# A planned attention and gMLP kernel: late weight loads moved behind the last key copy, GpSimd stepped by the planner as an engine of its own, smaller probability buffer, first query tile ahead of the first key tile

## The chip, the cores and the metric

The kernel runs on one core of one Trainium2 chip. The metric is the device time of one execution in microseconds (us); lower is better. Engines are named as in the profile: PE is the tensor engine (PEld its weight loads), ACT the scalar engine, DVE the vector engine, POOL is GpSimd, and SP only issues DMAs (SPq is its queue). PSUM is the matmul's output memory, in eight banks of 512 float32 columns.

## The reference

```python
# S = 2048 tokens, D = 512, 32 heads of 16; one key head and one value head for all
q = (x @ wq) in 32 heads; k = x @ wk; v = x @ wv          # k, v: [2048, 16]
a = softmax(q k^T / 4) v, heads side by side, @ wo
z = gelu(x @ w_in); z1, z2 = z[:, :688], layernorm(z[:, 688:])
b = (z1 * (w_sp @ z2 + b_sp)) @ w_out                     # w_sp: [2048, 2048]
out = sigmoid(x . gate_w) * a + (1 - sigmoid(x . gate_w)) * b
```

The attention has 32 x 2048 x 2048 scores, and each needs an exponential.

## The kernel before, in words

**Units and blocks.** The attention is cut into 32 units. A unit is 512 queries (chunk c = unit // 8) and four heads, one per group of 32 partitions. Units come in pairs that share one tile of queries, `QA`; the second unit of a pair reads its heads 16 partitions further down. That is why the keys stand twice in `KA`: `KA[:, 0]` comes from the key projection, and `KA[:, 1]` is the same data shifted by 16 partitions, which a DMA makes from `KA[:, 0]` (`ld_K1`, line 306, one DMA for each of the four chunks of 512 keys). Odd units read the shifted copy. A block is one head's 512 queries against 128 keys: one score matmul (`ps<-QA,KA`), 128x512 values. There are 64 blocks in a unit, 2048 in all.

**Two ways to the exponential.** Most blocks go to ACT, which takes the exponential of two (sometimes three or one) PSUM banks in one instruction (line 804) into `P`, a ring of `PB` tiles of 512 columns. Other blocks, up to eight key tiles of each unit, go to DVE in batches of four: `A` (line 816) reads the scores from PSUM and writes a linear function of them to `UW[:, 0]`; `u` (line 823) squares it in place; `W` (line 829) squares once more into `UW[:, 1]`. The rest of the polynomial is done by PE, with sums of the keys and values (`KTV`, `SVB`) made once. W reads and writes SBUF alone, so POOL may do it too; POOL then takes pieces of 256 columns, one or two at a time, and DVE takes what is left. PE multiplies P, u and W by the values (`ps<-P,V`, `ps<-UW,V`, `ps<-UW,VW`) into one PSUM bank, and these matmuls run four at a time on 32 columns each (a round).

**After a unit.** DVE transposes the unit's sums (`T1`, line 841) and takes the reciprocal of the row sums; POOL scales a pair of units (`Tn`, line 869) into a buffer for the whole chunk; when a chunk's eight units are done, SP issues a DMA transpose of it into `OT` (`t2_dma`, line 877). PE multiplies `OT` by `wo` in the output groups `g_out`, with the gMLP part of the same rows.

**The gMLP branch** fills PE between the attention's steps: z2 and z1 from `win`, gelu on ACT in one stretch (187 to 211 us), layernorm statistics and scaling on DVE (lines 635 and 649), and then, for each of four chunks of 512 rows, the product with `w_sp` (`g_sp`, line 687 on DVE). Its right side `wT` is loaded by four DMA transposes for each chunk (`ld_wT`, line 339). The next chunk's four are put on SP when the last product of the chunk before has been planned, and they overwrite what that product reads.

**The order of the work** is made by a planner in the Python code, before anything runs. It keeps a clock for PE, ACT and DVE, and always steps the engine whose clock is furthest behind: `pe_step`, `act_step` and `dve_step` choose the next instruction by rules and costs in ns and write it to that engine's list. `T[...]` holds the time at which the planner believes something ready. Every engine then runs its list strictly in order, with semaphores for the true dependences. So a belief of the planner that is wrong is paid as a wait, and everything behind the waiting instruction in its engine's list waits as well. Some beliefs that matter here: a shifted key copy is ready 2.95 us after the planner sends it to SP (`ld_K1`: 650 ns of SP's time and 2300 ns), whatever else stands in SP's list; `OT` is ready 7 us after `Tn` (`C_T2`).

**SP's list.** DMAs of one list issue in order, and an instruction that waits holds all behind it. `sp_dma` chains by default: each such DMA waits until the one chained before it has landed. The loads of `wo` (eight DMAs), `wout` and the first `wT` (`ld_wo`, `ld_rest`) are put on SP in `done` of `g_KTV` (lines 588 to 595).

**POOL in the planner.** `pool_try` is called only at the start of a DVE step. It looks at how much PSUM reading DVE has ahead of it (`psum_work`); while DVE reads PSUM, POOL may use SBUF without meeting DVE's two-input squares. A piece of two (512 columns) is given when that work is at least 1000 ns, a piece of one at 560 ns, only after 64 us of the plan, and not between the start of the gelu stretch and the end of the layernorm. `lock` makes the planner charge a DVE square for what is left of a POOL instruction.

Of the kernel before, what the change touches and what calls it, by code (L numbers as in the profile page):

```python
# [22 lines left out]
LN_EPS = 1e-5  # L23
PB = 19
ND = 5
# [12 lines left out]
DBK = (5, 4)  # L38
# [14 lines left out]
WPOOL = True  # L53
C_PW = 1000.0
C_ZN = 1200.0
ZP = ()
C_PH = 580.0
# [112 lines left out]
def build_kernel(nc, x_d, wq_d, wk_d, wv_d, wo_d, win_d, wsp_d, bsp_d, wout_d, gw_d, out_d):  # L170
    es = ExitStack()
    with es:
# [35 lines left out]
        rc = sb("rc", [128, 2, 16], F32)  # L208
        Tn = sb("Tn", [128, 2, 512], B16)
        OT = sb("OT", [128, 2, 16, 128], B16)  # L210
# [34 lines left out]
        TB = [outsb[:, :, :].rearrange("p k n -> p (k n)"), winf[:, 0:2048], winf[:, 2048:4096], winf[:, 0:2048]]  # L245
        TBK = [[("ob", k) for k in range(4)], ["W0"], ["W1"], ["W0"]]
        OT3 = winf[:, 4096:4608]
        wo3 = winf[:, 4608:5120]
# [195 lines left out]

        def g_K(c, lo=0, hi=512, b=BM):
            key = "K0a" if c == XO[0] and lo == 0 else ("K0", c)

            def piece(dt):
                return lambda: fm(b, hi - lo, 0, wk_rep[:, dt, :], xT[:, dt, 512 * c + lo:512 * c + hi], dt == 0, dt == 3, ["wk_rep", ("x", c)], "K")

            def ev():
                op("dve", lambda v: v.tensor_copy(KA[:, 0, 512 * c + lo:512 * c + hi], bank(b, hi - lo)), r=[bkey(b)], w=[key], tag="Kev")
# [15 lines left out]
            return Group([((hi - lo) / 2.4 + 2.6, piece(dt)) for dt in range(4)], [(68.0 + (hi - lo) / 0.96, ev)], lambda: when(("x", c)), done, bank=b, tag="K")  # L468

# [104 lines left out]
        def g_KTV():  # L574
            n0 = NKT - NMAX

            def piece(k, e):
                def f():
                    for q in range(4):
                        o = 512 * BM + 32 * NMAX * e  # L580
                        mm(ps[32 * q:32 * q + 32, o:o + 32 * (k + 1)], KN[:, k, e, :], V1[:, n0 + k:n0 + k + 1, :].broadcast_to([128, k + 1, 32]), k == NMAX - 1, k == 0,
                           ["KN", ("V", (n0 + k) // 4)], [bkey(BM)], tp=(0, 32 * q), tag="KTV")
                return f

            def ev():
                op("dve", lambda v: v.tensor_scalar(KF, bank(BM, 64 * NMAX).rearrange("p (e k w) -> p k e w", e=2, w=32), Q_C1, None, ALU.mult),
                   r=[bkey(BM), ("z1", 5)], w=["KF"], tag="KTVev")

            def done(t):
                for q in range(4):  # L590
                    op("sp", lambda d, q=q: d.dma_start(KTV[32 * q:32 * q + 32, :, :, q, :], KF[32 * q:32 * q + 32, :, :, :]),  # L591
                       r=["KF", ("z1", 5)], w=[("KTV", q)], dma=16, after=[o_ktv], tag="KTV")
# [253 lines left out]
        def norm_ops(pgx, c, jp, jjs, b0=0, b1=16, t1k=None, eng="dve", big=False):  # L846
# [16 lines left out]
            def d():  # L863
                dst = TB[c].rearrange("p (b z j w) -> p z j b w", z=4, j=2, w=16)[:, jp, :, :, :] if big else tnv[:, pr, j0:j1, b0:b1, :]
                aft = list(pgx.ops["dve"][-2:-1]) if eng == "pool" else []
                if big and c and jp == 0:
# [3 lines left out]
                                                      rc[:, j0:j1, b0:b1].unsqueeze(3).broadcast_to([128, n, nb, 16]), ALU.mult),  # L870
                       r=t1k + [("rc", j, b0) for j in jjs], w=TBK[c] if big else [("Tn", pr, j, b0) for j in jjs],
                       after=aft, tag="Tn")
# [77 lines left out]
        for i, c in enumerate(XO):  # L950
# [643 lines left out]
        def lock(now):  # L1594
            return max(0.0, plc["lock"] - now)

        def poly_step(now, only, full=False, idle=False):
            av = sum(w_avail(m, now) for m in pq)
            for m in sorted(pq):
# [3 lines left out]
                if ud < hd // 2 and th <= now and not (full and hd // 2 - ud < 2 and ud == 0):  # L1603
                    c_ = 65.0 + 0.5208 * 1024 * (hd // 2 - ud) + lock(now)
                    d_u(m, ud, hd // 2)
# [17 lines left out]
                c_ = 65.0 + 0.5208 * 256 * n + lock(now)  # L1623
                d_w("dve", m, wb, wb + n)
                uw_add(m, 1, wb, wb + n, now + c_ + D_END + L_X)
# [16 lines left out]

        def pool_try(now):
            if plc["free"] > now:
                return
            w = psum_work(now)
            for x in pl_q:
                if qt(x) > now:
                    continue
                if x[0] > 400.0 and w < pr["WIN"] and qt(x) > now - 6000.0:  # L1650
                    continue
# [6 lines left out]
                return  # L1658
            nh = 2 if w >= pr["WIN"] else 1 if w >= pr["WIH"] else 0
            if not WPOOL or now < 64000.0 or not nh or gst["arm"] and T.get("z2n", 1e12) > now:  # L1660
                return
            for m in sorted(pq):
# [5 lines left out]
                d_w("pool", m, i - n, i, after=pg.ops["dve"][-2:-1])  # L1668
                c_ = C_PW if n == 2 else C_PH
                plc["lock"] = now + c_  # L1670
# [15 lines left out]

        def dve_step(now):
            pool_try(now)
            if t1_q and qt(t1_q[0]) <= now:
# [58 lines left out]

        step = {"pe": pe_step, "act": act_step, "dve": dve_step}
        busy = {"pe": 0.0, "act": 0.0, "dve": 0.0}  # L1750
        log = []
        idle = 0
        last_end = {}
        while True:
            eng = min(free, key=lambda e: free[e])
            now = free[eng]
            clk["now"] = now
            r = step[eng](now)
            if r is not None:
                busy[eng] += r - now  # L1760
# [195 lines left out]
```

## Time and profile before

| | us |
|---|---|
| median of 3 runs (748.27 to 748.70) | 748.63 |
| the profiled execution's own time | 748.98 |
| its span, first to last instruction | 747.2 |
| busy: PE / ACT / DVE / POOL | 714.1 / 708.7 / 704.9 / 471.3 |
| idle of ACT ahead of its exponentials (27.0), of which waiting for PE | 26.7 |

The profile is of one execution. Busy is the time in which an engine has an instruction in flight; PE's is modelled from issue and latency, so its 96% is not PE at its peak. The span leaves out 1.8 us around the execution. A line number names a line of the kernel before; in the changed kernel the same code stands some 13 lines lower from `g_K` on. Rows of the program's order (marked order) hold no time: they only tell what stands behind what on an engine.

### The profile page before, as it was taken

Reading aid. Unit: us, or ns where it says so; the run is one execution under the profiler, and the core shown is the slowest. Engines: PE = TensorE matmul, PEld = TensorE weight load, DVE = VectorE, ACT = ScalarE, POOL = GpSimd, SP = SyncE. Lnnn points to the kernel's source line nnn. Section 1 sums busy time; section 2 is a strip of 40 time slices with the busy share of each in tenths; the row PEclk is TensorE's granted clock in tenths of the full one; section 3 lists DMA queues with packets and bytes.
Section 4 is the critical chain, followed back from the end, with each engine's and each line's share of the span. In section 5 each row is a group of like instructions: output and inputs, shape, how many; then the busy total and the mean of one; then the engine's idle time right before and its main releaser. Section 6 shows DMA issues by size and latency. Waiting matters only on the chain.

```text
span 747.2 us, 21846 instructions
## 1 busy us (share of the span) xinstructions
PE 714.1 (96%) x9048; PEld 210.7 (28%) x9048; DVE 704.9 (94%) x1035; ACT 708.7 (95%) x757; POOL 471.3 (63%) x440
## 2 busy tenths in 40 slices
PE   8927999999999999999999999999999999999996
PEld 3302322232432222322222232222223222222322
DVE  6934999999999999999999999999999999999996
ACT  5936999999999999999999999999999999999995
POOL 5520376766037876667777677756767776677772
PEclk9977999999999999999999999999999999999999
DMA  8441000000001000150000105000001510000101
GB/s 156 133 113 36 1 2 2 2 2 1 3 2 27 4 2 2 30 100 9 9 1 2 38 2 128 9 10 2 1 2 23 109 36 8 2 2 2 31 1 33
DMA packets 59810, 20.12 MB, mean 27 GB/s; under 512 B 54804, under 2 KB 59192, under 8 KB 59704
## 3 DMA queue, kind: packets, MB, share of 16 engines
q1 hardware_dynamic: 57448, 18.36, 11.0%
q8 instruction: 73, 1.20, 0.6%
q10 hardware_dynamic: 2256, 0.30, 0.2%
q14 instruction: 33, 0.27, 0.1%
HBM read 3.38 MB, written 2.10 MB: 7 GB/s over the span
## 4 chain that ended last, share of the span: by engine, by line
PE 69%; DVE 11%; ACT 10%; DMA 4%; issue 4%; SPq 1%; ACTq 0%; DVEq 0%
PE ps L377 69%; ACT P L804 9%; DVE UW L816 4%; DVE bst L635 2%; DMA wT<-in_B_w_sp_dram 2%; DVE UW L823 2%; DVE UW L829 1%; DMA wout<-in_B_w_out_dram 1%; DVE z L649 1%; DMA xT<-in_A_x_dram 1%; SPq L591 0%; SPq L318 0%; DMA KA<-KA 0%; ACT z L629 0%; DMA wo<-in_A_wo_dram 0%
## 5 line engine op out<-in xcount | busy, mean ns | idle before, releaser
L804 ACT ACTIVATE P<-ps 128x1024 bf16<-128x1024 f32 (+1 forms) x738 | 683.5, 1185 | 27.0 <-PE ps L377 26.7
L829 POOL TENSOR_TENSOR UW<-UW 128x512 f16<-128x512 f16 (+1 forms) x300 | 375.4, 1251 | 156.1 <-DVE UW L829 63.8
L816 DVE TENSOR_SCALAR UW<-ps 128x512 f16<-128x512 f32 (+1 forms) x423 | 351.0, 851 | 2.6 <-PE ps L377 1.9
L377 PE MATMUL ps<-QA,KA 32*128 32x512 bf16 x2048 | 313.6, 385 | 23.2 <-DMA KA<-KA 18.1
L377 PE MATMUL ps<-P,V 128*32 128x512 bf16 x1488 | 204.7, 386 | 0.4 <-issue 0.3
L823 DVE TENSOR_TENSOR UW<-UW 128x2048 f16<-128x2048 f16 (+1 forms) x176 | 177.9, 1011 | 1.3
L377 PEld LDWEIGHTS ps<-QA,KA 32*128 32x128 bf16 x2048 | 86.1, 91 | 325.6 <-ACT P L804 151.7
L377 PE MATMUL ps<-UW,VW 128*32 128x512 f16 x560 | 119.5, 384 | 0.0
L377 PE MATMUL ps<-wT,z 128*32 128x512 bf16 (+1 forms) x1536 | 116.3, 366 | 0.0
L829 DVE TENSOR_TENSOR UW<-UW 128x1024 f16<-128x1024 f16 (+4 forms) x176 | 109.0, 634 | 1.9 <-POOL UW L829 1.9
L377 PE MATMUL ps<-UW,V 128*32 128x512 f16 x560 | 83.9, 387 | 0.7 <-DVE UW L823 0.4
L377 PEld LDWEIGHTS ps<-P,V 128*32 128x32 bf16 x1488 | 46.8, 94 | 53.7 <-issue 48.7
L377 PEld LDWEIGHTS ps<-wT,z 128*32 128x32 bf16 x1536 | 28.2, 94 | 40.9 <-issue 40.4
L510 POOL TENSOR_TENSOR QSQ<-QA 128x512 bf16<-128x512 bf16 x16 | 25.7, 1609 | 19.8 <-DVE z L649 8.6
L621 DVE CAST z<-ps 128x344 bf16<-128x344 f32 x32 | 16.2, 506 | 21.2 <-PE ps L377 21.1
L377 PEld LDWEIGHTS ps<-UW,VW 128*32 128x32 bf16 x560 | 27.9, 94 | 17.3 <-issue 14.5
L377 PE MATMUL ps<-wout,z 128*32 128x512 bf16 x384 | 31.9, 384 | 0.0
L377 PE MATMUL ps<-win,xT 128*32 128x344 bf16 x512 | 30.6, 317 | 0.2 <-DVE km L488 0.2
L377 PEld LDWEIGHTS ps<-UW,V 128*32 128x32 bf16 x560 | 19.9, 95 | 19.6 <-issue 14.9
L472 POOL TENSOR_TENSOR KSQ<-KA 128x512 bf16<-128x512 bf16 x4 | 5.6, 1408 | 31.3 <-PE ps L377 31.2
L841 DVE STREAM_TRANSPOSE T<-ps 128x512 f32<-128x512 f32 (+1 forms) x33 | 22.7, 691 | 1.4 <-PE ps L377 1.3
L377 PE MATMUL ps<-QA,KTV 128*32 128x512 bf16 x128 | 23.3, 383 | 0.0
(114 smaller groups left out, 384.1 us busy)
## 6 DMA issues: line engine op xcount, KB each, us to landing
out_dram<-outsb SPq DMA_DIRECT2D x15, 128.0 KB, 1.7
win<-in_B_w_in_dram SPq DMA_DIRECT2D x1, 1376.0 KB, 7.5
wout<-in_B_w_out_dram SPq DMA_DIRECT2D x1, 640.0 KB, 4.2
wo<-in_A_wo_dram SPq DMA_DIRECT2D x8, 64.0 KB, 2.5
KA<-KA SPq DMA_DIRECT2D x4, 112.0 KB, 2.6
UW<-in_A_wq_dram SPq DMA_DIRECT2D x1, 384.0 KB, 4.1
wT<-in_B_w_sp_dram SPq DMA_TRANSPOSE x16, 4.4
UW<-in_A_wq_dram ACTq DMA_DIRECT2D x1, 128.0 KB, 3.9
```

The lines of the kernel that those rows point to most:

```text
L377: return t.matmul(dst, lhsT, rhs, start=start, stop=stop, tile_position=tp)
L472: op("pool", lambda g: g.tensor_tensor(KSQ[:], KA[:, 0, 512 * c:512 * c + 512], KA[:, 0, 512 * c:512 * c + 512], ALU.mult), r=[("K0", c), ...
L510: dq(pl_q, 1050.0, lambda: op("pool", lambda v: v.tensor_tensor(QSQ[:, q % 2, :], QA[:, q % NQ, :], QA[:, q % NQ, :], ALU.mult), r=[("Q", ...
L621: ev = lambda: op("dve", lambda v: v.tensor_copy(z2[:, FH * st + 344 * h:FH * st + 344 * h + 344], bank(BM, 344)), r=[bkey(BM)], w=[("z2", ...
L635: dq(dve_q, 410.0, lambda st=st, h=h: op("dve", lambda v: v.bn_stats(bst[:, st, h, :], z2[:, FH * st + 344 * h:FH * st + 344 * h + 344]), ...
L649: op("pool" if st in ZP else "dve", lambda v: v.tensor_scalar(z2[:, FH * st:FH * st + FH], z2[:, FH * st:FH * st + FH], mv[:, st, 0:1], rs ...
L804: op("act", lambda a: a.activation(P[:, 512 * p0:512 * (p0 + n)], ps[:, 512 * b0:512 * (b0 + n)], ACT.Exp), r=[bkey(b0 + i_) for i_ in ran ...
L816: op("dve", lambda v: v.tensor_scalar(UW[:, 0, s, 512 * i:512 * (i + n)], bank(b, 512 * n), Q_A, Q_AS, ALU.mult, ALU.add), r=[bkey(b + j) ...
L823: op("dve", lambda v: v.tensor_tensor(src, src, src, ALU.mult), r=k, w=k, tag="dTT")
L829: op(eng, lambda v: v.tensor_tensor(UW[:, 1, s, 256 * a:256 * b], src, src, ALU.mult), r=[("U", s, h) for h in range(a // 2, (b + 1) // 2) ...
L841: return lambda: pgx.op("dve", lambda v: v.transpose(T1[:, jj, c0:c1], bank(BO, c1 - c0, c0)), r=[bkey(BO)], w=[("T1", jj, c0)], tag="T1")
```

## The change

1. **Late loads.** `ld_wo` and `ld_rest` leave `done` of `g_KTV`. They are now called by `ld_late`, which counts two events: `done` of `g_KTV`, and `done` of the last chunk of keys, after that chunk's `ld_K1`.
2. **POOL as a fourth engine of the planner.** A new `pool_step` runs whenever POOL's clock is the furthest behind; it gives POOL nothing while DVE runs a square, and otherwise counts the rest of DVE's current instruction as cover. Pieces go up to four (1024 columns) at 184 + 428 ns per 256 columns, if DVE's PSUM work is at least that less 50 ns. Pieces are allowed from 45 us of the plan, and inside the gelu and layernorm stretch.
3. **Smaller ring, earlier products.** `PB` goes from 19 to 16 tiles, and the rule by which PE takes P products even in rounds that aren't full (`PRESS`) starts at 6 free tiles and not at 5. `Tn`, used for the last unit pair only, loses its own buffer and takes part of `win`.
4. **Start.** PE's list begins with the first query tile and then the first 128 keys, which go to another bank and are copied to `KA` by ACT, not by DVE.

```diff
-PB = 19
+PB = 16
...
-C_PW = 1000.0
+C_P0 = 184.0
+C_P1 = 428.0
...
-PR = dict(HALF=100.0, IDR=10, IDN=4, WRES=16, D_HG=2500.0, D_FL=False, WIN=1000.0, WIH=560.0, BACK=32, PRESS=5, FLEX=5000.0, RMIN=32, WBL=0.5, W_MIN=0.9, HOLD=0.0, RLEND=0)
+PR = dict(HALF=100.0, IDR=10, IDN=4, WRES=16, D_HG=2500.0, D_FL=False, WIN=1000.0, WIH=560.0, BACK=32, PRESS=6, FLEX=5000.0, RMIN=32, WBL=0.5, W_MIN=0.9, TTR=0.0, PMX=4, WMX=1000.0, PTO=6000.0, PSL=50.0, WP0=45000.0, WG=0, HOLD=0.0, RLEND=0)
...
+        lates = [2]
+
+        def ld_late():
+            lates[0] -= 1
+            if not lates[0]:
+                sp_dma(ld_wo, w=["wo"], n=128)
+                ld_rest()
...
                 elif hi == 512 and c == XO[3]:
                     ld_K1(c, t)
                     ld_bsp(0)
+                    ld_late()
...
                 T["KTV"] = t + 6000.0
-                sp_dma(ld_wo, w=["wo"], n=128)
-                ld_rest()
+                ld_late()
...
-        first = deque([g_K(XO[0], 0, 128), g_Q(0, DBK[0]), g_K(XO[0], 128, 512), g_V(XO[0], BO), g_K(XO[1]), g_V(XO[1], BO), g_K(XO[2]), g_V(XO[2]),
+        first = deque([g_Q(0, DBK[0]), g_K(XO[0], 0, 128, EB[1][0], True), g_K(XO[0], 128, 512), g_V(XO[0], BO), g_K(XO[1]), g_V(XO[1], BO), g_K(XO[2]), g_V(XO[2]),
...
+        def pool_step(now):
+            if plc["free"] > now:
+                return plc["free"]
+            rem = max(0.0, free["dve"] - now)
+            if dcur["tt"] and rem > pr["TTR"]:
+                return None
+            pool_try(now, rem)
+            return plc["free"] if plc["free"] > now else None
...
-            nh = 2 if w >= pr["WIN"] else 1 if w >= pr["WIH"] else 0
-            if not WPOOL or now < 64000.0 or not nh or gst["arm"] and T.get("z2n", 1e12) > now:
+            if not WPOOL or now < pr["WP0"] or pr["WG"] and gst["arm"] and T.get("z2n", 1e12) > now:
+                return
+            nh = 0
+            while nh < pr["PMX"] and w >= C_P0 + C_P1 * (nh + 1) - pr["PSL"]:
+                nh += 1
+            if not nh:
                 return
```

**First place: SP's list, from the load of `win` to the first `wT`.** This is one piece of the difference (- before, + changed, neither: both). `KTV<-z` is the placing of the key-value sums, `KA<-KA` a shifted key copy.

```order
 L306 DMA KA<-KA 112x512 x3
 L312 DMA win<-in_B_w_in_dram 128x4x1376
-L591 DMA KTV<-z 32x16x32 x4
+L605 DMA KTV<-z 32x16x32 x4
+L306 DMA KA<-KA 112x512
+L315 DMA bspz<-in_B_b_sp_dram 1x512
 L318 DMA wo<-in_A_wo_dram 16x4x512 x8
 L345 DMA wout<-in_B_w_out_dram 128x5x512
 L347 DMA wout<-in_B_w_out_dram 48x512 x2
 L339 DMA_TRANSPOSE wT<-in_B_w_sp_dram 128x16x128 x4
-L306 DMA KA<-KA 112x512
-L315 DMA bspz<-in_B_b_sp_dram 1x512
```

The fourth key copy and the first `bspz` moved ahead of the fifteen late loads.

**Second place: SP's list around the last four `wT` loads**, again one piece of the difference. `OT<-win` is the DMA transpose of a finished chunk of the attention, here of chunk 2 (the upper one in each version) and chunk 3; `out_dram` are finished rows.

```order
-L877 DMA_TRANSPOSE OT<-win 128x16x128
+L712 DMA out_dram<-outsb 128x512 x4
 L339 DMA_TRANSPOSE wT<-in_B_w_sp_dram 128x16x128 x4
 L315 DMA bspz<-in_B_b_sp_dram 1x512
-L699 DMA out_dram<-outsb 128x512 x4
-L877 DMA_TRANSPOSE OT<-win 128x16x128
-L1874 TENSOR_LOAD flag
-L1878 COMPARE_AND_BRANCH
+L890 DMA_TRANSPOSE OT<-win 128x16x128
+L712 DMA out_dram<-outsb 128x512 x4
+L890 DMA_TRANSPOSE OT<-win 128x16x128
```

The transpose of chunk 2 stood ahead of the last four `wT` loads and now stands behind them and their `bspz`.

**Third place: POOL's list around the layernorm's power (`rstd`)**, before and changed apart. `UW<-UW` are POOL's pieces of W, `QSQ` the squares of a query tile, `gtmp` and `good` a range check of a unit.

```order
81 L829 TENSOR_TENSOR UW<-UW 128x512 x4
82 L829 TENSOR_TENSOR UW<-UW 128x256
83 L644 TENSOR_TENSOR rstd<-ve,nhalf 128x16
84 L510 TENSOR_TENSOR QSQ<-QA 128x512
85 L829 TENSOR_TENSOR UW<-UW 128x512 x2
```

```order
100 L842 TENSOR_TENSOR UW<-UW 128x512 x2
101 L842 TENSOR_TENSOR UW<-UW 128x256 x10
102 L524 TENSOR_TENSOR QSQ<-QA 128x512
103 L657 TENSOR_TENSOR rstd<-ve,nhalf 128x16
104 L842 TENSOR_TENSOR UW<-UW 128x256 x5
105 L842 TENSOR_TENSOR UW<-UW 128x512
106 L842 TENSOR_TENSOR UW<-UW 128x256
```

Pieces of W now stand directly ahead of `rstd` and directly behind it, where the layernorm's scaling runs on DVE. Over the whole program POOL's pieces go from 180 of 512 columns and 120 of 256 to 169 of 512, 140 of 256, 32 of 768 and 3 of 1024; ACT's exponentials from 720 of two banks, 15 of three and 3 of one to 729, 7 and 1; DVE's batches from 140 to 142, and of W it keeps 140,800 columns where it had 163,840.

More of the change, by code (lines that the diff above doesn't have):

```diff
@@ L451, in ev @@
             def ev():
-                op("dve", lambda v: v.tensor_copy(KA[:, 0, 512 * c + lo:512 * c + hi], bank(b, hi - lo)), r=[bkey(b)], w=[key], tag="Kev")
+                if on_act:
+                    op("act", lambda a: a.activation(KA[:, 0, 512 * c + lo:512 * c + hi], bank(b, hi - lo), ACT.Copy), r=[bkey(b)], w=[key], tag="Kev")
+                else:
+                    op("dve", lambda v: v.tensor_copy(KA[:, 0, 512 * c + lo:512 * c + hi], bank(b, hi - lo)), r=[bkey(b)], w=[key], tag="Kev")
             def done(t):
@@ L467, in done @@
                         early.append(g_k2(c2))
-            return Group([((hi - lo) / 2.4 + 2.6, piece(dt)) for dt in range(4)], [(68.0 + (hi - lo) / 0.96, ev)], lambda: when(("x", c)), done, bank=b, tag="K")
+            gr = Group([((hi - lo) / 2.4 + 2.6, piece(dt)) for dt in range(4)], [(68.0 + (hi - lo) / 0.96, ev)], lambda: when(("x", c)), done, bank=b, tag="K")
+            gr.on_act = on_act
+            return gr
         def g_k2(c):
@@ L870, in d @@
                                                       rc[:, j0:j1, b0:b1].unsqueeze(3).broadcast_to([128, n, nb, 16]), ALU.mult),
-                       r=t1k + [("rc", j, b0) for j in jjs], w=TBK[c] if big else [("Tn", pr, j, b0) for j in jjs],
+                       r=t1k + [("rc", j, b0) for j in jjs], w=TBK[c] if big else [("Tn", pr, j, b0) for j in jjs] + ["W1"],
                        after=aft, tag="Tn")
@@ L1649, in pool_try @@
                     continue
-                if x[0] > 400.0 and w < pr["WIN"] and qt(x) > now - 6000.0:
+                if w < min(x[0] - pr["PSL"], pr["WMX"]) and qt(x) > now - pr["PTO"]:
                     continue
@@ L1747, in d_done @@
             return None
-        step = {"pe": pe_step, "act": act_step, "dve": dve_step}
-        busy = {"pe": 0.0, "act": 0.0, "dve": 0.0}
+        step = {"pe": pe_step, "act": act_step, "dve": dve_step, "pool": pool_step}
+        free["pool"] = 19000.0
+        busy = {"pe": 0.0, "act": 0.0, "dve": 0.0, "pool": 0.0}
         log = []
@@ L1758, in build_kernel @@
             r = step[eng](now)
+            if r is not None and eng == "pool":
+                free[eng] = r
+                continue
             if r is not None:
```

19 lines of the change are left out of this document (13 added, 6 removed).

## The prediction

> **What bounds the kernel now.** I read the page first, then the timelines of SP, PE and ACT around its one hole, then the stretch after it. The page's span, busy times and two of its slice rows (40 slices of 18.7 us; a digit is the busy share in tenths):
>
> ```profile
> span 747.2 us, 21846 instructions
> PE 714.1 (96%) x9048; PEld 210.7 (28%) x9048; DVE 704.9 (94%) x1035; ACT 708.7 (95%) x757; POOL 471.3 (63%) x440
> ACT  5936999999999999999999999999999999999995
> PEclk9977999999999999999999999999999999999999
> ```
>
> ACT is the engine to count by: outside the first slices and the last it is full. The stretch from 240 to 720 us says so exactly (PE, PEld, DVE, ACT, POOL busy, with instructions, then granted clock):
>
> ```profile
> 240.00:720.00 480.00, 479.80 (x5780) 134.01 (x5776) 475.84 (x656) 479.97 (x523) 345.15 (x297) 1.00 0.10 23
> ```
>
> ACT is busy 479.97 of 480 us with 523 instructions, 0.918 us for each; DVE has 4.2 us free there. So I count in ACT time: what ACT loses waiting or gains in work moves the end. The hole is in the third and fourth slice. The timelines of SP, PE and ACT over it (start, duration, engine and line, operation; in brackets the idle time before it and its releaser):
>
> ```profile
> 25.52 3.41 SPq L591 DMA_DIRECT2D KTV<-z  x4
> 28.98 3.90 SPq L318 DMA_DIRECT2D wo<-in_A_wo_dram  x8
> 34.82 0.39 SPq L345 DMA_DIRECT2D wout<-in_B_w_out_dram  x1
> 39.03 2.08 SPq L347 DMA_DIRECT2D wout<-in_B_w_out_dram  x2
> 42.50 14.98 SPq L339 DMA_TRANSPOSE wT<-in_B_w_sp_dram  x4
> 57.53 0.59 SPq L306 DMA_DIRECT2D KA<-KA  x1
> ```
> ```profile
> 41.81 0.38 PE L377 MATMUL ps<-QA,KA 32*128 32x512 bf16 x1
> 60.30 0.60 PE L377 MATMUL ps<-QA,KA 32*128 32x512 bf16 x1 [18.10 <-DMA KA<-KA]
> ```
> ```profile
> 60.94 1.02 ACT L804 ACTIVATE P<-ps 128x1024 bf16<-128x1024 f32 x1 [17.84 <-PE ps L377]
> 62.94 1.45 ACT L804 ACTIVATE P<-ps 128x1536 bf16<-128x1536 f32 x1 [0.98 <-PE ps L377]
> 64.89 1.02 ACT L804 ACTIVATE P<-ps 128x1024 bf16<-128x1024 f32 x1 [0.50 <-PE ps L377]
> 66.87 9.21 ACT L804 ACTIVATE P<-ps 128x1024 bf16<-128x1024 f32 x9 [0.96 <-PE ps L377]
> ```
>
> The fourth key copy stood behind fifteen loads, each chained to the landing of the one before, and left SP at 57.53. PE stood at its first score matmul on that copy for 18.10 us, ACT for 17.84. The three short waits after it, 0.98 + 0.50 + 0.96 = 2.44 us, belong to it too, as the clock shows (the windows' PEclk is the third number from the end):
>
> ```profile
> 42.00:46.00 4.00, 0.19 (x1) 0.00 (x0) 2.19 (x3) 1.10 (x1) 2.71 (x2) 0.98 0.53 114
> 60.00:63.00 3.00, 2.71 (x20) 0.64 (x24) 0.00 (x0) 1.08 (x2) 0.00 (x0) 0.50 0.02 6
> 63.00:66.00 3.00, 3.00 (x34) 1.00 (x26) 0.75 (x2) 2.41 (x2) 0.00 (x0) 0.50 0.00 0
> 66.00:70.00 4.00, 4.00 (x59) 1.24 (x51) 3.56 (x6) 3.13 (x3) 1.04 (x1) 0.96 0.00 0
> ```
>
> A mean of 0.98 over 42 to 46 puts the fall to one half at 45.8, 3.6 us after PE's last matmul ended at 42.2; 0.96 over 66 to 70 puts the return at 66.3. So PE restarted 6 us long at half clock and ACT starved on. The hole is worth 17.84 + 2.44 = 20.3 us of ACT.
>
> **The late loads.** With the new list the fourth copy follows the KTV DMAs, whose issue ends at 25.52 + 3.41 = 28.93. A key copy lands this long after its issue (view of its line):
>
> ```profile
> DMA to landing us min/median/max: 2.3/2.6/3.6
> ```
>
> So it is there by 31.6 to 32.6. PE wants it as its 711th matmul, the 709th before, which it reached at 42.2: 9.6 us to spare, and the wait goes whole. The fifteen loads start about 3 us later and have cover: `wT` is first read after the layernorm, past 220 us, `wo` and `wout` later still. KTV keeps its place. Term: -20.3 us; if the short waits weren't the clock's, -17.8.
>
> **What is late next.** The planner puts the transpose of chunk 2 (`OT<-win`) behind the last four `wT` loads. These overwrite what the third spatial product reads, so SP stands until that product's last matmul; then the four go one landing at a time, and `bspz` waits for the last. Before, the same loads took (SP's timeline):
>
> ```profile
> 576.06 1.94 SPq L877 DMA_TRANSPOSE OT<-win  x1
> 580.55 16.45 SPq L339 DMA_TRANSPOSE wT<-in_B_w_sp_dram  x4
> 599.36 0.26 SPq L315 DMA_DIRECT2D bspz<-in_B_b_sp_dram  x1
> ```
>
> That is 18.8 us from the first issue to `bspz`, and 0.3 until SP is free. The transpose then lands after (view of `OT`):
>
> ```profile
> DMA to landing us min/median/max: 3.6/4.4/4.7
> ```
>
> With 0.5 us from the last matmul's start to the first issue, `OT` is ready 0.5 + 18.8 + 0.3 + 4.4 = 24.0 us after the product's last matmul. PE gets to the first `wo` matmul of these rows sooner: in its new list 52 score matmuls stand between, and with 2048 of them over 737 exponentials (2.78 each) that is 18.7 exponentials of 0.918 us, 17.2 us. PE waits 6.8 us, with the queued score matmuls behind it, and ACT and DVE behind those. The planner doesn't see it: it believes in 7 us after `Tn`. By the hole above ACT loses 0.3 less than PE: 6.5 us. An idle of that length passes the 3.6 us after which the clock fell, so I add the 2.4 us of the restart. Term: +8.9; from 4.7 (a 5 us wait, no fall) to 10.3 (8 us and the fall).
>
> The Trainium skill, "TensorE: Matmul & The Clock Gate", Part 1, says that the window of about 3.4 us runs freely and that a whole idle one halves the clock. The fall at 3.6 us agrees with it; by that rule a wait of 6.5 us holds a whole window in some nine cases of ten, and the sum would be 0.2 us lower.
>
> **The planner's new split.** The page's groups (count, then busy us and mean ns, then idle before):
>
> ```profile
> L804 ACT ACTIVATE P<-ps 128x1024 bf16<-128x1024 f32 (+1 forms) x738 | 683.5, 1185 | 27.0 <-PE ps L377 26.7
> L816 DVE TENSOR_SCALAR UW<-ps 128x512 f16<-128x512 f32 (+1 forms) x423 | 351.0, 851 | 2.6 <-PE ps L377 1.9
> L823 DVE TENSOR_TENSOR UW<-UW 128x2048 f16<-128x2048 f16 (+1 forms) x176 | 177.9, 1011 | 1.3
> L829 DVE TENSOR_TENSOR UW<-UW 128x1024 f16<-128x1024 f16 (+4 forms) x176 | 109.0, 634 | 1.9 <-POOL UW L829 1.9
> L621 DVE CAST z<-ps 128x344 bf16<-128x344 f32 x32 | 16.2, 506 | 21.2 <-PE ps L377 21.1
> ```
>
> ACT had 1488 blocks (720 x 2 + 15 x 3 + 3), 0.459 us each, and has 1480: -3.7 us. Bounds: 0, if DVE or PE can't keep up with the shifted split, and -5, as fewer of the slow lone three-bank ones remain. DVE: A and u grow by 142/140, (351.0 + 177.9) x 0.0143 = +7.6; W shrinks from 163,840 to 140,800 columns, 109.0 x 0.141 = -15.3; together -7.7, 697.2 busy. Its idle was 42.3 us, 21.1 of it the hole; 697.2 + 21.2 = 718.4, against ACT's 708.7 - 3.7 + (38.5 idle - 20.3) = 723.2. DVE has 4.8 us in hand, which covers some more contention with POOL, so I cost the 44 added POOL pieces and the longer ones at nothing. The smaller ring leaves PE six free tiles, three exponentials, before it hurries, where it left five; rounds of fewer than four matmuls go from 73 to 78 of some 1775: nothing.
>
> **The start.** Here PE did 56 of the value matmuls ahead of the first scores and does 24 now, 32/56 of this row:
>
> ```profile
> 8.20 0.64 PE L377 MATMUL ps<-wvg,xT 128*32 128x33 bf16 x56
> ```
>
> That is -0.4 us, if ACT's copy of 128 keys, beside DVE's copy of the queries, is no later; between -0.6 and +0.3.
>
> **Sum.** For the profiled execution: 748.98 - 20.3 + 8.9 - 3.7 - 0.4 = 733.5. The median is 0.35 below it: **733 us**.
>
> **Rivals.**
>
> *B, the transpose isn't late* (0.20): `OT` lands before PE needs it, because PE comes later than 17 us or the loads finish sooner. Then 733 - 8.9 = 724. Against it stand the 18.8 us above, for it that PE's distance is worked out and not seen.
>
> *C, the layernorm is held up by POOL* (0.12). Pieces of W now run where POOL had stopped. The row of that scaling, and a collision that the trace does show (DVE's square beside POOL's key squares, then one of the same size alone):
>
> ```profile
> L649 DVE TENSOR_SCALAR z<-z,mv,rstd 128x688 bf16<-128x688 bf16 x16 | 6.1, 449 | 0.0
> 77.99 2.06 DVE L823 TENSOR_TENSOR UW<-UW 128x2048 f16<-128x2048 f16 x1
> 80.57 1.21 DVE L829 TENSOR_TENSOR UW<-UW 128x2048 f16<-128x2048 f16 x1
> 77.31 1.65 POOL L472 TENSOR_TENSOR KSQ<-KA 128x512 bf16<-128x512 bf16 x1 [8.72 <-PE ps L377]
> ```
>
> The square took 0.85 us more. The planner keeps POOL's pieces off squares but not off these scalings. If six of the sixteen are held as long, +5 us: 738. The Trainium skill, "SBUF — State Buffer", "Who interferes with whom", has a rule against the change here: a copy or `tensor_scalar` in a two-port mode and GpSimd shut each other out for a whole instruction, as do GpSimd's reads and a DVE instruction with two SBUF inputs. The square's row agrees; whether the scaling is such a case, no row shows.
>
> *D, POOL slows DVE's squares all along* (0.03): slower than before. It decides once DVE loses its 4.8 us in hand and the 15.6 of gain, 20.4 us, or 24 holds of 0.85 us. If each of the 35 pieces above 512 columns holds one, 29.8 us, the time is 733 + 29.8 - 4.8 = 758. Against it: 300 pieces now cost little, since the full squares' mean is near the lone 1.21 us:
>
> ```profile
> L823 DVE TENSOR_TENSOR UW<-UW 128x2048 f16<-128x2048 f16 x104 | 128.2, 1233 | 0.9
> ```
>
> *E, the copy is late all the same* (0.02), behind something on SP that I overlooked: 733 + 20.3 = 753.
>
> **Chances and range.** The forecast has 0.63; with its terms' bounds it reaches from 727 to 740. B ends at 724, a little less with the full -5. The range of 723 to 740 holds the forecast, nearly all of B and most of C, and leaves out D, E and a badly held layernorm. About 0.2% (1.5 us) is what a measurement of this kernel can tell from no change. Faster by more than that are the forecast, B and C, 0.95; within it 0.01, on D's way up; slower 0.04, D and E.
>
> **What would show it.** Right: the wait on `KA<-KA` is gone and the fourth copy issues near 29 us; the clock is full from 5 us on but for one short fall after about 570 us; ACT idles some 6 us before one exponential there, with PE waiting on `OT<-win`. B is right if PE shows no wait on `OT`; C if the scalings' mean rises well above 449 ns with ACT idle near 200 us; D if the full squares' mean rises above 1.4 us. Wrong altogether: ACT busy for more than 706 us, or idle spread in small pieces over the whole run.

## The result, and the profile after

| | before | after |
|---|---|---|
| median, us | 748.66 (748.27 to 749.78, 4 runs) | 739.38 (738.32 to 740.09, 4 runs) |
| ratio, 95% interval | | 0.9872 [0.9855, 0.989] |
| the profiled execution, its span | 748.98, 747.2 | 738.32, 736.5 |
| ACT busy, idle in the span | 708.7, 38.5 | 706.5, 30.0 |

The changed kernel is 9.3 us (1.3%) faster. The forecast was 733 in a range of 723 to 740. The interval of the ratio excludes 733: 739.4 is 6.4 us above the forecast and 0.6 us below the upper end of the range. The page's span, busy times and the same two slice rows:

```profile
span 736.5 us, 21958 instructions
PE 711.5 (97%) x9056; PEld 208.9 (28%) x9056; DVE 703.6 (96%) x1031; ACT 706.5 (96%) x757; POOL 525.1 (71%) x484
ACT  5999999999989999999999999999999599999995
PEclk9999999999999999999999999999999899999999
```

The hole of the third and fourth slice is gone. A new one stands in the 32nd slice, and a small dent in the 12th. SP's timeline, around the first place of the change and around the second:

```profile
25.61 2.72 SPq L605 DMA_DIRECT2D KTV<-z  x4
28.40 0.60 SPq L306 DMA_DIRECT2D KA<-KA  x1
...
43.91 17.12 SPq L339 DMA_TRANSPOSE wT<-in_B_w_sp_dram  x4
...
556.90 16.98 SPq L339 DMA_TRANSPOSE wT<-in_B_w_sp_dram  x4
576.41 0.26 SPq L315 DMA_DIRECT2D bspz<-in_B_b_sp_dram  x1
576.77 1.88 SPq L890 DMA_TRANSPOSE OT<-win  x1
```

The fourth key copy leaves at 28.40 where it had left at 57.53. The transpose of chunk 2 leaves at 576.77, 19.9 us after the first of the loads that now stand ahead of it. ACT's timeline shows what each dent costs (in brackets the idle time before the row):

```profile
202.58 2.85 ACT L817 ACTIVATE P<-ps 128x1024 bf16<-128x1024 f32 x3 [0.45 <-PE ps L377]
206.88 1.02 ACT L817 ACTIVATE P<-ps 128x1024 bf16<-128x1024 f32 x1 [1.45 <-PE ps L377]
208.33 1.02 ACT L817 ACTIVATE P<-ps 128x1024 bf16<-128x1024 f32 x1 [0.42 <-PE ps L377]
210.34 364.71 ACT L817 ACTIVATE P<-ps 128x1024 bf16<-128x1024 f32 x397 [0.98 <-PE ps L377]
582.28 1.02 ACT L817 ACTIVATE P<-ps 128x1024 bf16<-128x1024 f32 x1 [7.23 <-PE ps L377]
583.86 1.02 ACT L817 ACTIVATE P<-ps 128x1024 bf16<-128x1024 f32 x1 [0.56 <-PE ps L377]
585.31 1.02 ACT L817 ACTIVATE P<-ps 128x1024 bf16<-128x1024 f32 x1 [0.43 <-PE ps L377]
```

From 210 to 575 us, 397 exponentials run almost without a gap (ACT is busy 364.52 of 364.71 us). At 582 ACT loses 7.23 + 0.56 + 0.43 us and, ahead of the next row, 0.30: 8.5 us. At 202 to 210 it loses 0.45 + 1.45 + 0.42 + 0.98 = 3.3 us that it did not lose before. The groups name what PE waited for and what became slower:

```profile
L817 ACT ACTIVATE P<-ps 128x1024 bf16<-128x1024 f32 (+1 forms) x737 | 681.2, 1126 | 14.7 <-PE ps L377 14.1
L377 PE MATMUL ps<-wo,OT 128*32 128x512 bf16 x256 | 23.1, 399 | 7.0 <-DMA OT<-win 7.0
L662 DVE TENSOR_SCALAR z<-z,mv,rstd 128x688 bf16<-128x688 bf16 x16 | 8.6, 600 | 0.0
L836 DVE TENSOR_TENSOR UW<-UW 128x2048 f16<-128x2048 f16 x103 | 128.8, 1251 | 1.0
```

PE waits 7.0 us for `OT<-win`. The layernorm's scalings take 600 ns where they had taken 449. The full squares are where they were (1251 against 1233).

### The profile page after: what moved, and what is told of

It is laid out like the page before. It is cut to its first block, busy times and chain, and to the rows that moved or that the text cites. A ratio compares the mean times of both kernels' runs of the same rounds, so it can differ in the third digit from the quotient of the medians.

```text
span 736.5 us, 21958 instructions
## 1 busy us (share of the span) xinstructions
PE 711.5 (97%) x9056; PEld 208.9 (28%) x9056; DVE 703.6 (96%) x1031; ACT 706.5 (96%) x757; POOL 525.1 (71%) x484
## 4 chain that ended last, share of the span: by engine, by line
PE 60%; ACT 17%; DVE 15%; issue 5%; DMA 1%; POOL 1%; ACTq 0%; POOLq 0%; DVEq 0%
PE ps L377 60%; ACT P L817 16%; DVE UW L829 7%; DVE UW L836 3%; DVE UW L842 2%; DVE z L662 1%; POOL UW L842 1%; DMA xT<-in_A_x_dram 1%; DVE T L854 1%; DMA OT<-win 1%; DVE bst L648 0%; DVE z L634 0%; DVE z L700 0%; ACT z L642 0%; ACT L642 0%
## 5 line engine op out<-in xcount | busy, mean ns | idle before, releaser
L817 ACT ACTIVATE P<-ps 128x1024 bf16<-128x1024 f32 (+1 forms) x737 | 681.2, 1126 | 14.7 <-PE ps L377 14.1
L842 POOL TENSOR_TENSOR UW<-UW 128x512 f16<-128x512 f16 (+2 forms) x344 | 431.2, 1253 | 151.0 <-DVE UW L842 47.6
L829 DVE TENSOR_SCALAR UW<-ps 128x512 f16<-128x512 f32 (+1 forms) x435 | 355.9, 841 | 13.9 <-PE ps L377 13.4
L377 PE MATMUL ps<-P,V 128*32 128x512 bf16 x1480 | 214.0, 385 | 0.2 <-DVE KN L548 0.2
L836 DVE TENSOR_TENSOR UW<-UW 128x2048 f16<-128x2048 f16 (+1 forms) x181 | 181.5, 1005 | 1.3
L377 PEld LDWEIGHTS ps<-QA,KA 32*128 32x128 bf16 x2048 | 82.0, 91 | 305.2 <-ACT P L817 136.1
L377 PE MATMUL ps<-UW,VW 128*32 128x512 f16 x568 | 124.8, 384 | 0.7 <-POOL UW L842 0.7
L842 DVE TENSOR_TENSOR UW<-UW 128x1024 f16<-128x1024 f16 (+5 forms) x156 | 97.4, 638 | 1.1 <-POOL UW L842 1.0
L377 PEld LDWEIGHTS ps<-P,V 128*32 128x32 bf16 x1480 | 50.7, 94 | 55.3 <-issue 50.2
L377 PE MATMUL ps<-wo,OT 128*32 128x512 bf16 x256 | 23.1, 399 | 7.0 <-DMA OT<-win 7.0
L377 PEld LDWEIGHTS ps<-UW,V 128*32 128x32 bf16 x568 | 20.3, 94 | 20.7 <-issue 13.8
L377 PE MATMUL ps<-CT,SVB 128*32 128x512 bf16 x128 | 22.9, 383 | 0.0
```

What stands on the lines that cost most here:

```text
L377: return t.matmul(dst, lhsT, rhs, start=start, stop=stop, tile_position=tp)
L817: op("act", lambda a: a.activation(P[:, 512 * p0:512 * (p0 + n)], ps[:, 512 * b0:512 * (b0 + n)], ACT.Exp), r=[bkey(b0 + i_) for i_ in ran ...
L829: op("dve", lambda v: v.tensor_scalar(UW[:, 0, s, 512 * i:512 * (i + n)], bank(b, 512 * n), Q_A, Q_AS, ALU.mult, ALU.add), r=[bkey(b + j) ...
L836: op("dve", lambda v: v.tensor_tensor(src, src, src, ALU.mult), r=k, w=k, tag="dTT")
L842: op(eng, lambda v: v.tensor_tensor(UW[:, 1, s, 256 * a:256 * b], src, src, ALU.mult), r=[("U", s, h) for h in range(a // 2, (b + 1) // 2) ...
```

## The experiments

My theory after these two traces: the late loads are the whole gain; the late transpose takes a good part of it back; and the planner's new split is worth its 2 to 4 us but is eaten in the layernorm. Three sets of kernels were run. The kernel before took 749.07, 749.73 and 750.29 us beside them, so numbers of different sets are compared by their ratio to it.

**1. The late loads alone** (set 1): the kernel before with part 1 of the change.

```diff
                     ld_bsp(0)
+                    ld_late()
...
                 T["KTV"] = t + 6000.0
-                sp_dma(ld_wo, w=["wo"], n=128)
-                ld_rest()
+                ld_late()
```

> The kernel before with the late loads alone moved behind the last key copy; planner, ring, start and POOL as before. Theory (the hole is worth 20.3 us of ACT and nothing takes its place, since here the transpose of chunk 2 stays ahead of the last wT loads): 748.7 - 20.3 = 728.4 us, 727 to 730; no wait on a key copy, granted clock full throughout. Rival (the hole hides other waits that come out when it goes): 732 us or more.

Measured: 727.92 (727.59 to 727.95), ratio 0.971 [0.9689, 0.973]. The page's span, busy times and its ACT row:

```profile
span 726.1 us, 21847 instructions
PE 711.6 (98%) x9048; PEld 210.8 (29%) x9048; DVE 704.7 (97%) x1035; ACT 708.1 (98%) x757; POOL 471.4 (65%) x440
ACT  5999999999999999999999999999999999999995
```

No dent is left, ACT is busy as before (708.1 for 708.7), and 21.1 us are gone, within what was expected. One edit of a few lines beats the whole change by 11.5 us (12 by the ratios).

**2. The transpose ahead of the loads** (set 1): the changed kernel, with only SP's list altered; the second piece stands in `t2_dma`, behind the transpose.

```diff
-                    ld_wT(tc + 1)
+                    if ("OT", tc) in T:
+                        ld_wT(tc + 1)
+                    else:
+                        wt_late.append(tc)
...
+            if c in wt_late:
+                ld_wT(c + 1)
```

> The whole change, but the last four wT loads are put on SP only after the transpose of chunk 2; every other list is the same. Theory (that wait costs the 7.2 us and the three short ones behind it, 8.5 us in all): 739.4 - 8.5 = 730.9 us, 730 to 732; no wait on OT. Rival (ACT or DVE makes part of it good later, or the next load is late instead): 734 us or more.

Measured: 728.68 (727.92 to 729.25), ratio 0.9718 [0.9697, 0.9739], spans 736.5 to 727.4. One place in SP's list was worth 9.1 us by the spans, 10.7 by the medians and 11.5 by the ratios. The median lies 1.3 us below the 730 to 732 expected: the 8.5 us of the trace go with the pair of profiled executions, which are the fastest of the changed kernel's four and the slowest of this run's. With it put right the changed kernel stands level with the late loads alone: everything else in the change, together, brings nothing. Its page and its groups:

```profile
PE 710.2 (98%) x9056; PEld 209.0 (29%) x9056; DVE 703.7 (97%) x1031; ACT 706.2 (97%) x757; POOL 524.9 (72%) x484
```
```profile
L821 ACT ACTIVATE P<-ps 128x1024 bf16<-128x1024 f32 (+1 forms) x737 | 680.8, 1129 | 5.9 <-PE ps L377 5.2
L663 DVE TENSOR_SCALAR z<-z,mv,rstd 128x688 bf16<-128x688 bf16 x16 | 8.6, 599 | 0.0
```

ACT works 1.9 us less than in run 1 and idles 21.2 us instead of 18.0: 3.2 more, with the scalings at 599 ns and the waits at the layernorm still there.

**3. No POOL pieces in the gelu and layernorm stretch** (set 1): run 2's kernel with `WG=0` set to `WG=1`.

> As e2, and POOL gets no pieces of W between the start of the gelu stretch and the end of the layernorm (as before the change). Theory (POOL's pieces hold the layernorm's scalings and with them PE and ACT, 3.3 us of ACT): 727.6 us if DVE can take the squares back, up to 729.5 if not; mean of the scalings back near 450 ns, ACT idle under 1.5 us between 180 and 215 us. Rival (the idle there is the planner's own and not POOL's): 731 us, as e2.

Measured: 728.62 (728.39 to 728.73), ratio 0.9719 [0.9699, 0.974]. The scalings are back at 447 ns, and ACT's idle time at that place is down to some 0.5 us, as the theory had it. But the new plan gives ACT four blocks back and waits 4.58 us for 3.71 before the last rows, so the time is run 2's.

```profile
L821 ACT ACTIVATE P<-ps 128x1024 bf16<-128x1024 f32 (+1 forms) x740 | 682.4, 1125 | 3.4 <-PE ps L377 3.0
L663 DVE TENSOR_SCALAR z<-z,mv,rstd 128x688 bf16<-128x688 bf16 x16 | 6.1, 447 | 0.0
```

**4. The larger ring** (set 1): run 2's kernel with `PB = 19` and `PRESS=5`, as before the change.

> As e2, with the ring of 19 tiles and the limit of 5 free ones of before. Theory (the ring is no bound, ACT never waits on it): within 1.5 us of e2, 729.5 to 732.5. Rival (the smaller ring costs ACT time through uneven rounds): 727 to 729.

Measured: 732.08 (731.39 to 733.28), ratio 0.9772 [0.9749, 0.9794], 3.4 us slower than run 2 where I had allowed 1.5. So no cost of the smaller ring shows, as the prediction said. The larger one got a plan with a longer end: ACT waits 5.60 us for 3.71 before the last rows, which is most of the 2.1 us between the two spans (729.5 and 727.4).

**5. Everything but the late loads** (set 2): the changed kernel with the fifteen loads back ahead of the fourth key copy.

```diff
                     ld_bsp(0)
-                    ld_late()
...
-                ld_late()
+                sp_dma(ld_wo, w=["wo"], n=128)
+                ld_rest()
```

> The changed kernel with the late loads alone taken back: the fifteen loads are issued in done of g_KTV again, ahead of the fourth key copy; everything else is the changed kernel. Theory (the late loads are the whole gain, and the rest of the change costs the transpose's wait): the changed kernel's 739.4 plus the 21.1 that the late loads gave alone = 760.5, between 758 and 762, so over 1% slower than the kernel before; PE waits some 18 us on KA<-KA and some 7 to 8 us on OT<-win. Rival (the planner's engine, the split and the start are worth the 3.7 + 0.4 of the prediction after all and are hidden in the changed kernel by something else): 756 or less.

Measured: 764.25 (761.48 to 766.86), ratio 1.0185 [1.0164, 1.0206]. Without its first part the change is 1.9% slower than the kernel before. The theory holds in its sign, and the rival is out, but the value lies 2.3 us above the 758 to 762 expected (0.5 us, reckoned by the ratio to 748.66). In its trace the hole cost ACT 22.1 us, waits behind it included, for the 20.3 of before, and the layernorm 6.9 for 3.3, though here the scalings keep their pace. The groups of POOL in the window from 221 to 226 us, PE's timeline behind it, and the scalings' group:

```profile
L842 POOL TENSOR_TENSOR UW<-UW 128x256 f16<-128x256 f16 x1 | 4.5, 4451 | 1.3 <-DVE z L662 1.3
```
```profile
226.31 0.39 PE L377 MATMUL ps<-UW,VW 128*32 128x512 f16 x1 [3.12 <-POOL UW L842]
```
```profile
L662 DVE TENSOR_SCALAR z<-z,mv,rstd 128x688 bf16<-128x688 bf16 x16 | 6.2, 458 | 0.0
```

One piece of 256 columns took 4.45 us, from 221.80 to 226.25, just behind the end of DVE's last scaling (225.79), and PE waited 3.12 us for it. DVE's and POOL's lists are the changed kernel's, instruction by instruction. There POOL got through and the scalings lost (600 ns); here DVE got through (458 ns) and the piece lost. By these rows it is one collision that either side can lose; why it fell out this way here no trace shows.

**6. The late loads and the new start** (set 2): run 1's kernel with part 4 of the change.

```diff
-        first = deque([g_K(XO[0], 0, 128), g_Q(0, DBK[0]), ...
+        first = deque([g_Q(0, DBK[0]), g_K(XO[0], 0, 128, EB[1][0], True), ...
```

> The kernel before with the late loads and the new start (first query tile ahead of the first 128 keys, whose copy ACT makes); POOL's pieces, ring and PRESS are those of before. The late loads alone took 727.9. Theory (the start is worth what the first exponential's time shows, 9.62 to 8.96 us): 727.3, between 726 and 728.5, with the first exponential near 9.0 us. Rival (ACT's copy beside DVE's copy of the queries holds something up, or the other plan that follows from the start loses it again): 729 or more.

Measured: 729.83 (728.96 to 731.52), ratio 0.973 [0.9716, 0.9744]: 0.2% above run 1 by the ratios, whose intervals overlap: the theory's gain is missed, and the rival's 729 reached. The first exponential starts at 9.31 us against 9.62, so 0.3 us shows in this pair of traces; but the plan that follows loses more elsewhere, 1.8 us of it in four small waits at 43 to 48 us.

**7. No POOL pieces beside the scalings only** (set 2): run 2's kernel, with pieces kept out from the layernorm's power to its last scaling, and left in the gelu stretch.

```diff
                             t2 = clk["now"] + 4500.0
+                            gst["ln"] = True
...
-            if not WPOOL or now < pr["WP0"] or pr["WG"] and gst["arm"] and T.get("z2n", 1e12) > now:
+            if not WPOOL or now < pr["WP0"] or gst.get("ln") and T.get("z2n", 1e12) > now:
```

> The changed kernel with chunk 2's transpose ahead of the last four wT loads, as in the run of 728.7, and no POOL piece planned from the layernorm's power to the end of its scalings; POOL's pieces in the gelu stretch stay. Theory (ACT loses some 3 us there because POOL's pieces lengthen the scalings): the scalings' mean is back at 450 ns, ACT's idle falls from 21.2 to 18 us, and the time is 725.5, between 724.5 and 727. Rival (what isn't lost in the layernorm comes back as less shifted work, a longer tail or waits elsewhere, as when POOL was kept out of the gelu stretch as well): 728 or more.

Measured: 727.92 (727.74 to 731.38), ratio 0.9719 [0.9698, 0.9741], the same as run 2's. The scalings are back at 457 ns and the layernorm's waits are gone, as the theory said, but not the time, as the rival said. The 724.5 to 727 expected is missed. ACT's idle time falls to 19.8 us and not to 18: the plan has a new wait of 1.00 us at 684 us, and 4.83 us instead of 3.71 before the last rows.

**8. A placebo** (set 2): run 2's kernel with the planner's fixed cost of a POOL piece at 190 ns for 184.

> A placebo: the changed kernel with chunk 2's transpose ahead of the last four wT loads, and the planner's fixed cost of a POOL piece 190 ns in place of 184. No rule is changed, but some hundred choices of the plan fall out another way. Theory (differences of 1 to 3 us between these kernels are the scatter of plans, not the worth of a rule): it differs from 728.7 by 0.7 us or more, up to 3 either way. Rival (plans of the same rules are worth the same): within 0.5 of 728.7.

Measured: 730.54 (730.03 to 731.95), ratio 0.9749 [0.9734, 0.9763], above run 2 by 0.3% of 749, 2 us. No rule of the planner differs, and the intervals of the two ratios only just meet. So differences of 1 to 2 us between runs 1, 2, 3, 6 and 7 can't be put down to the rule that was changed; 4's 3.4 us is at the edge of that. One placebo gives the size of this scatter only roughly.

**9. The transpose put behind the loads in a kernel that has nothing else of the change** (set 3): run 1's kernel, one place in SP's list.

```diff
+            if c == 2 and ("wT", 3) not in T:
+                t2_held.append(lambda: op("sp", ...))      # issued after ld_wT(3)
```

> The kernel before with the late loads, and with one thing more: on SP the transpose of chunk 2 is put behind the last four wT loads and their bspz, where it stands in the changed kernel. Every other list is that of the run with the late loads alone (727.9). In that run's trace the spatial product's last matmul ends at 559.1, the loads are issued from 559.60 to bspz at 578.97 + 0.26, and PE reaches its first wo matmul of those rows at 565.96. Theory (the prediction's sum for a late transpose): OT is ready at 579.3 + 4.4 = 583.7, PE waits 17.7 us, ACT 17.4, and the clock's fall adds 2.4: 727.9 + 19.8 = 747.7, between 744 and 750. Rival (the changed kernel's wait was something of its new plan, or DMA transposes would have landed side by side): 735 or less.

Measured: 747.88 (746.64 to 751.79), ratio 0.9973 [0.9957, 0.9988]. SP's, PE's and ACT's timelines of it:

```profile
559.71 17.15 SPq L339 DMA_TRANSPOSE wT<-in_B_w_sp_dram  x4
578.91 0.26 SPq L315 DMA_DIRECT2D bspz<-in_B_b_sp_dram  x1
579.26 1.94 SPq L889 DMA_TRANSPOSE OT<-win  x1
```
```profile
583.57 1.04 PE L377 MATMUL ps<-wo,OT 128*32 128x512 bf16 x8 [17.43 <-DMA OT<-win]
```
```profile
585.25 1.02 ACT L815 ACTIVATE P<-ps 128x1024 bf16<-128x1024 f32 x1 [17.73 <-PE ps L377]
587.16 1.02 ACT L815 ACTIVATE P<-ps 128x1024 bf16<-128x1024 f32 x1 [0.88 <-PE ps L377]
```

`OT` was due at 583.7 and PE started at 583.57; the wait was to be 17.7 and is 17.43, the time 747.7 and is 747.9 in the median (by the ratios 19.7 us above run 1, for 19.8). That is the prediction's sum for a late transpose, borne out in another plan with another distance: here PE came 6.9 us after the product, in the changed kernel some 17. One term of it was too small in the profiled execution, which took 750.71: the seven waits behind the first add 3.8 us there, not 2.4.

**10. The disputed collision by itself** (set 3).

> A kernel that computes nothing of the reference (its output is zeros): DVE's and POOL's instructions by themselves and beside each other, in stretches parted by barriers. In order: 16 layernorm scalings (128x688) alone; 8 POOL pieces of 256 columns alone; 8 of 512 alone; 16 scalings beside 8 pieces of 256; 16 beside 8 of 512; 12 reads of PSUM (A, 512 columns) alone; 12 beside 6 pieces of 512; 8 full squares alone; 8 beside 8 pieces of 512. Theory (scaling and piece shut each other out of SBUF, and either may be the one that loses): alone 0.45 and 0.61 or 1.04 us; beside each other the scalings' mean passes 0.55, or the pieces of 256 pass 1.2, or both; A beside POOL stays at 0.69 and POOL near 1.04; the squares rise above 1.5. Rival (in the changed kernel the instructions were only longer by their place in the plan): scalings and pieces take the same alone and side by side, within 0.05 us.

DVE's timeline of it (one execution), where each row is a stretch after its first instruction, in the order of the expectation:

```profile
18.82 5.62 DVE L162 TENSOR_SCALAR z<-z,mv,rstd 128x688 bf16<-128x688 bf16 x15
40.57 8.17 DVE L162 TENSOR_SCALAR z<-z,mv,rstd 128x688 bf16<-128x688 bf16 x15
49.44 11.59 DVE L162 TENSOR_SCALAR z<-z,mv,rstd 128x688 bf16<-128x688 bf16 x15
61.96 6.66 DVE L166 TENSOR_SCALAR UW<-ps 128x512 f16<-128x512 f32 x11
69.55 6.66 DVE L166 TENSOR_SCALAR UW<-ps 128x512 f16<-128x512 f32 x11
77.79 8.79 DVE L170 TENSOR_TENSOR UW<-UW 128x2048 f16<-128x2048 f16 x7
88.16 13.81 DVE L170 TENSOR_TENSOR UW<-UW 128x2048 f16<-128x2048 f16 x7
```

POOL's rows of the same stretches: pieces of 256 alone and beside scalings, of 512 alone, beside scalings and beside squares.

```profile
24.93 5.46 POOL L175 TENSOR_TENSOR UW<-UW 128x256 f16<-128x256 f16 x8 [0.20 <-DVE bar L159]
30.94 8.87 POOL L175 TENSOR_TENSOR UW<-UW 128x512 f16<-128x512 f16 x8 [0.21 <-DVE bar L159]
40.37 5.60 POOL L175 TENSOR_TENSOR UW<-UW 128x256 f16<-128x256 f16 x8 [0.21 <-DVE bar L159]
49.24 9.02 POOL L175 TENSOR_TENSOR UW<-UW 128x512 f16<-128x512 f16 x8 [0.21 <-DVE bar L159]
87.06 15.80 POOL L175 TENSOR_TENSOR UW<-UW 128x512 f16<-128x512 f16 x8 [0.21 <-DVE bar L159]
```

Fifteen scalings take 5.62 us alone, 8.17 beside eight pieces of 256 columns and 11.59 beside eight of 512. So a piece costs DVE 0.32 or 0.75 us, and POOL itself loses next to nothing (5.46 to 5.60, 8.87 to 9.02). In both widths that is what the piece takes alone (0.68 and 1.11) less 0.36 us. Reads of PSUM lose nothing at all, 6.66 and 6.66. Squares and pieces both pay: 8.79 to 13.81, and 8.87 to 15.80. The theory holds; the rival, within 0.05 us, is out.

## Why the prediction was right, and where it was not

The terms, made against the profiled execution as the prediction made them:

| term | predicted | measured |
|---|---|---|
| late loads | -20.3 | -21.1 alone (run 1) |
| late transpose | +8.9 | +8.5 in ACT's timeline; +9.1 to +11.5 when undone (run 2) |
| planner's split | -3.7 | -2.3 (the group's 683.5 to 681.2) |
| POOL's added pieces | 0 | +3.3 at the layernorm |
| start | -0.4 | -0.3 (first exponential 9.26 to 8.96; over all traces, 9.54 to 9.08 in the mean) |

With the measured terms, and the -20.3 kept, 748.98 comes to 737.9; the execution took 738.32, where the sum had forecast 733.5. The two large terms were right in mechanism and size. The two that failed erred the same way, by 1.4 and 3.3 us, and the time stayed in the range with 0.6 us to spare; that end of it, 740, had been set for the terms' bounds and for most of rival C.

- **The hole: right, to its size.** The copy issued at 28.40, near the 29 forecast; the wait on `KA<-KA` and the half clock after it are gone. Run 1 shows that the wait has no successor worth naming, and that rival E is out.
- **The transpose: right, to its size.** PE's wait was 7.0 for 6.8. ACT's first wait was longer than I said (7.23 for 6.5) and the clock's share smaller (1.3 for 2.4), so two errors cancel in part in the term's 8.5 for 8.9. Its upper bound was added up wrongly: 8 - 0.3 + 2.4 is 10.1, not 10.3, and all the upper bounds together give 741, not 740. Runs 2 and 9 show the cause from both sides. Rival B is out.
- **The split: one step that failed.** "ACT had 1488 blocks, 0.459 us each, and has 1480" priced a block at the mean of the group. The count of instructions fell by one only, 738 to 737: eight of three banks and two of one went, and nine of two came. The eight blocks were worth 2.3 us, 0.29 each.
- **POOL's pieces: the other one.** "I cost the 44 added POOL pieces and the longer ones at nothing", with DVE's 4.8 us in hand as the cover. Part of the cover wasn't there: DVE's busy time fell by 1.3 us, 704.9 to 703.6, and not by 7.7. Its groups in the changed kernel are below; A and u took 8.5 us more for 7.6, W gave up 11.6 for 15.3, and the scalings took 2.5 more. And time in hand over a whole program is no cover at one place: in the layernorm the scalings are ahead of the first spatial product and of DVE's next reads of PSUM, for both of which PE waits. This is rival C, in the place and with the sign it named, at 3.3 us for its 5. Of these, 0.42 and 0.98 came while the granted clock stood at one half (206.7 to 210.1 us). I had set it *against* the forecast, as another way for it to go; the forecast's two mechanisms and C are not exclusive, and all three came true. The forecast with C's 5 us is the 738 that C named, 1.4 from the median.

```profile
L829 DVE TENSOR_SCALAR UW<-ps 128x512 f16<-128x512 f32 (+1 forms) x435 | 355.9, 841 | 13.9 <-PE ps L377 13.4
L836 DVE TENSOR_TENSOR UW<-UW 128x2048 f16<-128x2048 f16 (+1 forms) x181 | 181.5, 1005 | 1.3
L842 DVE TENSOR_TENSOR UW<-UW 128x1024 f16<-128x1024 f16 (+5 forms) x156 | 97.4, 638 | 1.1 <-POOL UW L842 1.0
```

- The Trainium skill, "SBUF — State Buffer", "Who interferes with whom", has the rule: a `tensor_scalar` in a two-port mode and GpSimd shut each other out for a whole instruction; a DVE instruction with two SBUF inputs meets a GpSimd instruction that reads SBUF; and outside the two-port modes one with at most one SBUF input doesn't meet GpSimd. Run 10 agrees on who meets whom: scalings 5.62 to 11.59, squares 8.79 to 13.81, PSUM reads 6.66 both ways. It doesn't show a scaling shut out for a whole piece, since each piece costs 0.36 us less than it takes. I had cited the rule and given C 0.12; but each of the five kernels with pieces beside the scalings (the changed one, runs 2, 4, 5 and 8) has waits of ACT there of 1 us and more, and runs 3 and 7, without such pieces, have none above 0.51.
- **D: out.** The full squares' mean is 1251 ns. Run 10 shows what pieces beside squares cost.
- **What the shifted work was worth.** Freed of the transpose the rest of the change gives nothing (run 2 against run 1). In the traces its 1.9 us of ACT work and the 0.5 of an earlier first exponential (9.62 to 9.10) are paid back by some 3 us of waits at the layernorm. Where that is mended (runs 3 and 7), the time isn't better by what was mended: the plan pays elsewhere, in blocks given back or in a longer end. By the placebo, plans of equal rules can differ by as much. So it is shown that the planner's part doesn't pay, and left open what a plan without collisions would give.
- **The signs.** One sign of "wrong altogether" was met: "ACT busy for more than 706 us", where the page has 706.5 (and 706.2 in run 2). It comes from the split's missing 1.4 us and left the two large mechanisms standing, so as a sign it was set too close. The clock was to fall once, after about 570 us; it fell at 206.7 as well.
- **Left open:** the profiled execution was the fastest of its four; the others took 0.7 to 1.8 us more, at a mean granted clock of 0.986 to 0.988 for 0.993, and no trace shows where.

The best kernel found is the one before with the late loads alone, 727.9 us. No combination beat it beyond the scatter.

## What to carry to other kernels

When one entry of an in-order DMA list moves, write out what now stands ahead of each entry that an engine waits for: the same list gave the 21 us (a small copy behind fifteen chained loads) and took 9 to 11 of it back (a transpose behind four). Price the work that an engine gives up by the form of instruction that goes, not by the group's mean; and look for the cover of added work at the place where it runs. Before a gain of 1 or 2 us is put down to a scheduler's rule, change a number in it that shouldn't matter, and see how far the time moves.

## What the runs showed of the hardware that I had not expected

A collision's loser isn't fixed. With the same lists, the scalings took 600 ns each in the changed kernel, and in run 5 a single piece that takes 0.61 us alone stood 4.45 us behind ten scalings in a row. In run 10, where nothing else ran, the scalings lost every time.

The granted clock also fell without a long wait. The windows of the changed kernel (PE busy is the second number, the clock the third from the end):

```profile
202.00:204.00 2.00, 2.00 (x25) 0.53 (x26) 2.00 (x5) 1.55 (x3) 1.34 (x2) 1.00 0.00 0
204.00:205.00 1.00, 0.59 (x10) 0.09 (x8) 1.00 (x2) 1.00 (x2) 0.60 (x1) 1.00 0.00 0
205.00:206.00 1.00, 0.00 (x0) 0.00 (x0) 1.00 (x2) 0.43 (x1) 0.61 (x1) 1.00 0.00 0
206.00:207.00 1.00, 0.64 (x8) 0.24 (x12) 0.96 (x3) 0.12 (x1) 0.62 (x1) 0.84 0.00 0
207.00:208.00 1.00, 1.00 (x10) 0.10 (x2) 1.00 (x3) 0.91 (x1) 0.93 (x1) 0.50 0.00 0
```

A mean of 0.84 over 206 to 207 puts the fall at 206.7. PE's longest pause there was 1.77 us, and in the 3.4 us up to the fall, from 203.3 on, it had been busy for over 1 us by the first two rows. In run 2 the clock fell in the same way at 207.7, again with no pause of PE above 1.77 us. At the transpose the clock fell at 578.7, 4.7 us after PE had stopped. The Trainium skill, "TensorE: Matmul & The Clock Gate", Part 1, speaks of a whole idle window of some 3.4 us: the fall at 578.7 agrees with it, the two at the layernorm came without one.
